# Six key-difference tasks 36 slots apart instead of eight 24 slots apart, weight pieces 24 slots apart, and other scan spacings, in a gated mix of attention and Fourier mixing

## The chip, the cores and the metric

The kernel runs on one core of a Trainium2 chip. The time is that of one execution on the device in microseconds (us), as the median of several runs. The engines are named as in the profile: PE multiplies matrices (PEld is its loading of weights), DVE is the vector engine, ACT the scalar (activation) engine, POOL the general-purpose engine, and SP is an engine that here only issues DMA transfers. Each engine runs its own queue of instructions strictly in the order in which they were written, and waits at an instruction until what it needs is there. ACT and POOL have DMA queues of their own.

## The reference, cut to what matters

The input `x` has 2048 rows of 512 numbers. Everything is float32.

```python
g = sigmoid((x * gate_w).sum(-1))
qkv = x @ wqkv                               # 32 heads of 16
p = softmax(q @ k.T * 16**-0.5)              # 2048 x 2048 for each head
a = (p @ v) @ wo
b = Cr @ (x @ Wr.T) - Ci @ (x @ Wi.T)        # Cr, Ci: 2048 x 2048; Wr, Wi: 512 x 512
out = g * a + (1 - g) * b
```

The projection weights are 64 times larger than usual, so the softmax needs the maximum of each row of scores before it takes exponents. The kernel therefore computes every score twice: once in a *scan* that keeps only maxima, and once for use.

## The kernel before, in words

**Precision.** The matrix engine takes a rounded 32-bit format. To keep accuracy an operand is split into a rounded part `hi` (ACT copies and so rounds) and a rest `lo` (POOL or DVE subtracts `hi` from the number), and a product is three products: hi·hi, hi·lo and lo·hi.

**Slots.** The first part of the program, the front, is written out as *products*, each of which is a pair of 64-row matmuls that run side by side (`halves_of`, L176). After each pair `beside` (L225) is called: that is one *slot*. A block of output, 128 rows by 512, takes 12 slots (24 matmuls). `beside` does two more things. It runs what is due: `after(n, f, ...)` (L203) puts a piece of work on a list, and the work is written into its engine's queue n slots later, in the order of due slot. And it writes scans at a set rate: `scan_at(s)` sets the spacing in slots. A scan of 128 queries against 512 keys for two heads is a pair of matmuls with 48 rows. It costs the matrix engine as much as one slot.

**Stages of the front**, by slot count: q projections up to slot 240, k projections to 384 (`project_t`, L366), values to 576 (`wv`), the two hidden Fourier products to 768 (`wr`) and to 960 (`wi`) (`project_s`, L394), and then the sequence Fourier product in 96 units of 12 slots to 2112. After the front come the exponents and the product with the values for all heads, with the rest of the scans, which the change does not touch.

**A block's way out.** In `project_s` the matmuls of a block leave two halves in a pair of PSUM banks, `xy`, of which there are two. ACT copies the halves to `tx` (one buffer) and `ty` (two buffers), L401 and L402. Four slots later POOL adds them to `ab` (L498), and seven slots after that SP stores `ab` to memory. In `project_t` the sum `s` is made by POOL, ACT rounds it to `eh`, POOL subtracts to `el`, and SP stores both; for keys SP also stores the plain sum to `ks_d` (L388), and for odd blocks of 512 rows `kf_d` as well.

**Weights.** `load_w` (L338) loads one 512x512 weight matrix in a single transfer and splits it in four pieces, the first `wait` slots later and the others each 12 slots after the one before: ACT rounds (L281), POOL subtracts (L282). Pieces fall at multiples of 12 slots.

**Folded scans.** From scan 192 to 691 (`FOLDED`) keys come in pairs. Each scan multiplies the queries either with the difference of two key blocks or with the second block; then max(a, b) = max(a - b, 0) + b. ACT takes max(., 0) of the difference (L153), and DVE adds the other and keeps the maximum (L155). Their rate is PACE/FOLD_PACE over the spacing that `scan_at` set: with spacing PACE one folded scan falls each FOLD_PACE slots. With spacing NARROW it is slower, and this holds in the first 24 slots of the sequence product and around the *swap*, the 120 slots from 1656 to 1776, in which the operand of the real part is replaced by that of the imaginary part, one of 16 pieces after the other (`renew`, L575: ACT rounds, DVE or POOL subtracts).

**Key differences.** `fold_keys(f, g)` (L348) makes the differences for one quarter `f` of the heads and one pair of key blocks. SP loads the two sums from `ks_d` into `a` and `b` (two buffers in all, the tag `el`), POOL subtracts (after 12 slots), ACT rounds to `fh` (17), POOL subtracts the rest into the buffer of `b` (18), and SP stores both to `kf_d` (19 and 23). The next task's load of `b` has to wait until the last store has read that buffer. There are eight such tasks, 24 slots apart, all in the `wr` stage; the first is written at slot 594. `load_scan_beside` (L217) reads what was stored, for the first time at slot 835. Quarter 3 of the heads is never scanned in folded form: the last folded scan, 691, belongs to pair 10 of the 16, and a quarter has four pairs.

Of the kernel before, what the change touches and what calls it, by code (L numbers as in the profile page):

```python
# [10 lines left out]
F32 = mybir.dt.float32  # L11
# [13 lines left out]
NB = S // P  # L25
ND = D // P
# [9 lines left out]
FRONT = 564 + 16 * LATER  # L36
PACE = 3.9
FOLDED = range(3 * SCANS, FRONT)
FOLD_PACE = 2.23
NARROW = 4.5  # L40
NWARM = 20
MIX = TOTAL - FRONT + 1
OUT = MIX + NB * LATER
# [3 lines left out]
def build(tc, x, xT, wqkv, wo, wrT, wiT, cr, ci, gate, out):  # L47
    nc = tc.nc
    with ExitStack() as ctx:
# [140 lines left out]
        with ExitStack() as pf:  # L190
# [8 lines left out]
            def xy():  # L199
                ps = psf.tile([P, 2, 512], F32, tag="xy", name="xy")  # L200
                return ps[:, 0, :], ps[:, 1, :]

            def after(n, f, *args):  # L203

                count[0] += 1
                due.append((slots[0] + n, count[0], f, args))
# [15 lines left out]
            def scan_at(spacing):  # L222
                pace[0] = spacing

            def beside():  # L225
# [3 lines left out]
                if pace[0] is None:  # L229
                    return  # L230
                pace[1] += (PACE / FOLD_PACE if seen[0] in FOLDED else 1.0) / pace[0]
                if seen[0] == FOLDED[0] and not beds:
# [39 lines left out]
            def products(ps, parts):  # L272
                n = 0
                for lhs, rhs in parts:
                    for a, b in ((0, 0), (0, 1), (1, 0)):
                        halves_of(ps, lhs[a], rhs[b], n == 0, n == 3 * len(parts) - 1)
                        n += 1
                        beside()
# [5 lines left out]
            def load_operand(ph, s, pool):  # L284
                raw = pool.tile([P, D], F32, tag="raw", name="abr", bufs=3)
                nc.sync.dma_start(raw, ab_d[ph][s])
                return raw
# [14 lines left out]
            def load_coef(n, raw):  # L302
                ph, t, u = coef[n]
                craw[n] = raw
                nc.sync.dma_start(raw, (cr, ci)[ph][t, :, u * CS:(u + 1) * CS, :])
# [11 lines left out]
            with ExitStack() as px:  # L317
# [20 lines left out]
                def load_w(w, src, wait, engine):  # L338

                    raw = stk.tile([P, ND, 512], F32, tag="stk", name="wraw")  # L340
                    nc.sync.dma_start(raw, src.rearrange("(d p) m -> p d m", p=P))
                    for d in range(ND):
                        after(wait + 12 * d, split_w, w, d, raw[:, d, :], engine)

                def split_x(d, c):
                    split(*xs[d, c], raws[d][:, c * 512:(c + 1) * 512], nc.vector)
# [1 line left out]
                def fold_keys(f, g):  # L348

                    a, b = (ep.tile([P, 512], F32, tag="el", name="fa") for _ in range(2))  # L350
                    c = 2 * g
                    for i, v in enumerate((a, b)):
                        nc.sync.dma_start(v, ks_d[f][:, (c + i) * 512:(c + i + 1) * 512])
                    hi = ep.tile([P, 512], F32R, tag="gb", name="fh", bufs=1)
                    lo = b.bitcast(F32R)

                    def store(i, v):
                        nc.sync.dma_start(kf_d[f][:, i, c * 512:(c + 1) * 512], v.bitcast(F32))

                    after(12, nc.gpsimd.tensor_sub, a, a, b)  # L360
                    after(17, nc.scalar.copy, hi, a)
                    after(18, nc.gpsimd.tensor_sub, lo, a, hi.bitcast(F32))
                    after(19, store, 0, hi)
                    after(23, store, 1, lo)

                def project_t(w, dst, f, c, ps=None):  # L366
                    ps = ps or xy()
                    products(ps, [([w[i][d][:, f * P:(f + 1) * P] for i in range(2)], xs[d, c])
                                  for d in range(ND)])
                    tx = ep.tile([P, 512], F32, tag="tx", name="tx", bufs=1)  # L370
                    folded = dst is k_d
                    s = ep.tile([P, 512], F32, tag="ty", name="s")
                    hi = ep.tile([P, 512], F32R, tag="eh", name="eh", bufs=3)
                    lo = ep.tile([P, 512], F32R, tag="el", name="el")
                    nc.scalar.copy(tx, ps[0])
                    if pace[0] is None:
                        after(5, nc.vector.tensor_add, s, ps[1], tx)
                    else:
                        nc.scalar.copy(s, ps[1])
                        after(5, nc.gpsimd.tensor_add, s, s, tx)  # L380

                    def store(i, v):
                        nc.sync.dma_start(dst[f][:, i, c * 512:(c + 1) * 512], v.bitcast(F32))
                        if folded and c % 2:
                            nc.sync.dma_start(kf_d[f][:, i, c * 512:(c + 1) * 512], v.bitcast(F32))

                    if folded:
                        after(10, nc.sync.dma_start, ks_d[f][:, c * 512:(c + 1) * 512], s)  # L388
                    after(9, nc.scalar.copy, hi, s)
                    after(10, nc.gpsimd.tensor_sub, lo, s, hi.bitcast(F32))  # L390
                    after(14, store, 0, hi)
                    after(20, store, 1, lo)

                def project_s(w, t, sign, use):  # L394
                    ps = xy()
                    q = slice((t % 4) * P, (t % 4 + 1) * P)
                    products(ps, [([v[:, q] for v in xs[d, t // 4]], [w[i][d] for i in range(2)])
                                  for d in range(ND)])
                    tx = ep.tile([P, 512], F32, tag="tx", name="tx", bufs=1)
                    ty = ep.tile([P, 512], F32, tag="ty", name="ty")  # L400
                    nc.scalar.mul(tx, ps[0], sign)  # L401
                    nc.scalar.mul(ty, ps[1], sign)  # L402
                    after(4, use, t, tx, ty)
# [43 lines left out]
                for n, (w, dst, f, c) in enumerate(order):  # L447
                    lead = s1() if n in (0, 2, 4, 6) else None
                    project_t(w, dst, f, c, lead and (lead[:, 0, :], lead[:, 1, :]))
# [3 lines left out]
                    project_t(wq, q_d, f, c)  # L453
                wv = new_w()
                for n, (f, c) in enumerate([(f, c) for f in range(1, ND) for c in range(NC)]):
                    if n == 3:
                        load_w(wv, wqkv[:, 1024:1536], 48, nc.gpsimd)
                    project_t(wk, k_d, f, c)

# [35 lines left out]
                def to_rhs(i):  # L495
                    def use(t, tx, ty):
                        ab = ep.tile([P, 512], F32, tag="eh", name="ab", bufs=3)
                        nc.gpsimd.tensor_add(ab, tx, ty)  # L498
                        after(7, nc.sync.dma_start, ab_d[i][t], ab)
                    return use  # L500

                for t in range(NB):
                    if t == 3:
                        load_w(wi, wiT, 48, nc.gpsimd)
                    if t % 2:
                        after(6, fold_keys, *divmod(t // 2, 2))
                    project_s(wr, t, 1.0, to_rhs(0))
                use = to_rhs(1)
                for t in range(NB):
                    if t > 3:  # L510
                        after(24, split_operand, t - 4, load_operand(0, t - 4, rp), nc.gpsimd)
                    if t == 8:
                        first = stk.tile([P, 4, CS, P], F32, tag="stk", name="first")
                        tail = stk.tile([P, 4, D], F32, tag="stk", name="tail")
                    if 8 <= t < 12:
                        load_coef(t - 8, first[:, t - 8])
                    if t >= 12:
                        nc.sync.dma_start(tail[:, t - 12, :], ab_d[0][t])
                    if t == 12:
                        scan_at(5.0)  # L520
                    if 12 <= t < 15:
                        after(4, prepare, t - 12, nc.scalar.copy, nc.vector.tensor_sub)
                    project_s(wi, t, -1.0, use)
                run_due(True)

            with ExitStack() as py:
# [9 lines left out]
                for d in range(4):  # L536
                    after(4 + 6 * d, split_operand, NB - 4 + d, tail[:, d, :], nc.vector if d < 2 else nc.gpsimd)
                scan_at(NARROW)
                after(24, scan_at, PACE)
# [9 lines left out]
                for n, (ph, t, u) in enumerate(coef):  # L549
                    prepare(n + 3)  # L550
                    fetch(n + 8)
                    if u == 0 and (ph, t) == (0, NB - 1):
                        scan_at(NARROW)
                    if u == 2 and (ph, t) == (1, 0):
# [6 lines left out]
                    hi, lo = ready.pop(n)  # L561
# [5 lines left out]
                    if (ph, t, u) == (0, NB - 3, 0):  # L567
                        for i in range(2):
                            raw = stk.tile([P, 4, D], F32, tag="stk", name="early")
# [437 lines left out]
```

## Time and profile before

| | |
|---|---|
| runs shown | median 1776.61 us (1775.0 to 1776.8) |
| profiled execution | 1772.7 us, of it 1770.9 us from the first to the last instruction |
| PE busy | 97% of the span |
| ACT, DVE, POOL busy | 82%, 65%, 40% |
| front: slots 0 to 2112 | about 5.8 to 717 us |
| values to the wr stage | slot 384 at 118.3 us, slot 576 at 175.7 us |
| wr stage, wi stage | slots 576 to 768 at 175.7 to 253.6 us, to 960 at 313.7 us |
| swap | slots 1656 to 1776 at 554.2 to 599.2 us |

The times of slots are read by counting the matmuls of L180 in the trace, two to a slot. In the profile, a share of PE busy near 100% says little by itself, as matmuls overlap; the number of matmuls or weight loads in a stretch says more. In the view by windows each engine has its busy time and, in brackets, the number of its instructions. In the chain of work that ended last, each line is a start, a length and what it was: an engine with the tile that it wrote and its line, or a DMA with what it moved. In the lists of waits, a line names who waited for whom, the sum in us, how often, and the longest one.

### The profile page before, as it was taken

How to read it: one execution, taken by the hardware profiler on the slowest of the kernel's cores; microseconds unless marked ns; L12 is line 12 of the kernel's file. 1: busy time of each engine (PE TensorE's matmuls, PEld its weight loads, DVE VectorE, ACT ScalarE, POOL GpSimd, SP SyncE). 2: the span in 40 equal slices, each digit the busy share in tenths (PEclk: the TensorE clock that was granted, in tenths of full speed). 3: DMA queues.
4: the chain of work that ended last, by engine and by line, in shares of the span. 5: the costliest groups of instructions: out<-in, count | busy, mean ns of one | idle time of the engine just before them, and what ended most of it. 6: DMA issues, size and time to landing. Idle time of an engine off the chain costs nothing.

```text
span 1770.9 us, 35629 instructions
## 1 busy us (share of the span) xinstructions
PE 1724.9 (97%) x13640; PEld 1032.9 (58%) x13640; DVE 1151.2 (65%) x1876; ACT 1451.5 (82%) x2386; POOL 716.4 (40%) x818
## 2 busy tenths in 40 slices
PE   8999879999999999999999999999999999999998
PEld 6877658898898788434333333333334555555554
DVE  6799869889989898666666666666664221122333
ACT  5445234788888788899999999999999888888885
POOL 3678556655555665123232323323232322222212
PEclk9999999999999999999999999999999999999999
DMA  8693657433335546341433332414413253254712
GB/s 296 216 335 89 190 156 220 132 113 107 114 121 180 155 129 136 69 74 29 93 59 61 58 66 55 88 35 78 90 31 71 69 118 91 70 137 123 183 42 98
DMA packets 128538, 202.69 MB, mean 114 GB/s; under 512 B 54208, under 2 KB 56752, under 8 KB 121456
## 3 DMA queue, kind: packets, MB, share of 16 engines
q1 hardware_dynamic: 86096, 164.17, 34.3%
q0 software_dynamic: 38496, 19.47, 5.2%
q10 hardware_dynamic: 3776, 16.78, 3.5%
q8 instruction: 107, 1.75, 0.4%
q14 instruction: 63, 0.52, 0.1%
HBM read 134.09 MB, written 65.81 MB: 113 GB/s over the span
## 4 chain that ended last, share of the span: by engine, by line
PE 86%; DMA 6%; DVE 2%; POOL 2%; issue 2%; ACT 1%; SPq 0%; DVEq 0%; POOLq 0%; ACTq 0%
PE pvb L658 28%; PE xy L180 20%; PE s L643 18%; PE s L180 8%; PE s L149 7%; PE s L130 6%; DMA fa<-ks_d 2%; DMA kf_d<-fa 1%; POOL fa L215 1%; DVE mx L132 1%; DMA raws<-xT 1%; DMA ks_d<-s 1%; DMA raws<-wqkv 0%; DMA q_d<-el 0%; POOL s L215 0%
## 5 line engine op out<-in xcount | busy, mean ns | idle before, releaser
L132 DVE TENSOR_REDUCE mx<-s 128x2 f32<-128x1024 f32 x524 | 628.8, 1223 | 228.9 <-PE s L130 227.7
L647 ACT ACTIVATE eb<-s 128x1024 f32<-128x1024 f32 x512 | 581.7, 1136 | 54.4 <-PE s L643 54.4
L651 ACT ACTIVATE e<-s 128x512 f32<-128x512 f32 x1024 | 612.7, 713 | 0.4 <-PE s L643 0.4
L658 PE MATMUL pvb<-e,va 128*17 128x512 f32 x2048 | 516.9, 598 | 0.0
L658 PE MATMUL pvb<-eb,va 128*17 128x512 f32 x2048 | 516.7, 598 | 0.0
L643 PEld LDWEIGHTS s<-qs,ks 50*128 50x128 f32 x2048 | 213.8, 185 | 372.3 <-ACT eb L647 282.6
L643 PE MATMUL s<-qs,ks 50*128 50x512 f32 x2048 | 427.8, 437 | 2.3 <-DVE ty L598 1.6
L155 DVE CUSTOM_DVE_ANT_0 fold<-s,fold 128x512 f32<-128x512 f32 x500 | 336.9, 690 | 42.2 <-PE s L149 20.0
L153 ACT ACTIVATE fold<-s 128x512 f32<-128x512 f32 x500 | 294.3, 602 | 70.0 <-PE s L149 51.4
L149 PE MATMUL s<-ks,qs 48*128 48x512 f32 x1000 | 236.0, 403 | 7.2 <-DVE mx L155 5.7
L130 PE MATMUL s<-ks,qs 48*128 48x512 f32 x1048 | 221.8, 398 | 4.4 <-DVE mx L132 2.9
L666 POOL DMA_DIRECT2D lc<-ob x124 | 62.9, 514 | 303.3 <-DVE ob L663 303.3
L658 PEld LDWEIGHTS pvb<-eb,va 128*17 128x17 f32 x2048 | 69.1, 95 | 188.3 <-issue 180.3
L149 PEld LDWEIGHTS s<-ks,qs 48*128 48x128 f32 x1000 | 129.0, 184 | 40.9 <-DVE mx L155 16.2
L673 POOL DMA_DIRECT2D r_d<-lc x31 | 18.1, 583 | 292.5 <-DVE lc L672 282.5
L130 PEld LDWEIGHTS s<-ks,qs 48*128 48x128 f32 x1048 | 107.8, 185 | 15.2 <-DVE mx L132 5.7
L180 PE MATMUL xy<-w,b 64*128 64x512 f32 x768 | 107.1, 396 | 2.7 <-ACT ty L402 2.4
L675 POOL DMA_DIRECT2D rb<-r_d x124 | 60.3, 494 | 68.7 <-DMA r_d<-lc 68.5
L180 PEld LDWEIGHTS xy<-w,b 64*128 64x128 f32 x768 | 74.9, 188 | 19.6 <-ACT ty L402 4.0
L752 DVE SCALAR_TENSOR_TENSOR y<-s,g,y 128x512 f32<-128x512 f32 x50 | 36.6, 748 | 76.4 <-PE s L180 75.8
L180 PE MATMUL s<-b,chi 64*128 64x512 f32 x542 | 85.2, 390 | 0.3 <-ACT chi L961 0.3
L401 ACT ACTIVATE tx<-xy 128x512 f32<-128x512 f32 x48 | 28.7, 597 | 65.9 <-PE xy L180 48.1
(750 smaller groups left out, 2365.8 us busy)
## 6 DMA issues: line engine op xcount, KB each, us to landing
craw<-ci SPq DMA_DIRECT2D x64, 256.0 KB
craw<-cr SPq DMA_DIRECT2D x60, 256.0 KB
ks<-k_d SPq DMA_DIRECT2D x46, 256.0 KB
qs<-q_d SPq DMA_DIRECT2D x46, 256.0 KB
ab_d<-ab SPq DMA_DIRECT2D x32, 256.0 KB
y_d<-y SPq DMA_DIRECT2D x32, 256.0 KB
o_d<-oh POOLq DMA_DIRECT2D x28, 256.0 KB, 9.4
o_d<-ol POOLq DMA_DIRECT2D x28, 256.0 KB, 12.7
```

What stands on the lines that cost most here:

```text
L130: nc.tensor.matmul(ps[:, j, :], qs[b:b + 48, qb * P:(qb + 1) * P], ks[b:b + 48, c * 512:(c + 1) * 512], start=True, stop=True)
L132: nc.vector.tensor_reduce(mx[p][:, :, qb, c], ps, axis=AX.X, op=ALU.max)
L149: nc.tensor.matmul(ps, qs[b:b + 48, qb * P:(qb + 1) * P], ks[b:b + 48, c * 512:(c + 1) * 512], start=True, stop=True)
L153: nc.scalar.activation(fold[j], ps, AF.Relu)
L155: nc.vector.tensor_tensor_reduce(out=fold[j], in0=ps, in1=fold[j], scale=1.0, scalar=-3.0e38, op0=ALU.add, op1=ALU.max, accum_out=mx[p][:, ...
L180: nc.tensor.matmul(ps[j], lhs[r], rhs[r], start=first, stop=last)
L643: nc.tensor.matmul(pss[j], ks[b:b + 50, kb * P:(kb + 1) * P], qs[b:b + 50, q0:q0 + 512], start=True, stop=True)
L647: nc.scalar.activation(e, ps, AF.Exp, scale=SCALE)
L651: nc.scalar.activation(e[j], pss[j], AF.Exp, scale=SCALE)
L658: nc.tensor.matmul(pvb[r:r + VC, :], va[:, kb, 2 * p + j, :], es[c][j], start=kb == 0, stop=kb == NB - 1, tile_position=(0, r))
L666: nc.gpsimd.dma_start(lc[32 * n:32 * n + 32, :], ob[r + DH:r + VC, :].rearrange("p (s e) -> p s e", e=16))
L675: nc.gpsimd.dma_start(rb[r:r + DH, :], r_d[p][h][n:n + 1, :].to_broadcast([DH, 512]))
```

## The change

Six things are edited.

- `fold_keys` is called six times, not eight: quarter 3 is left out, and five tasks are written in the `wr` stage at every third block, the sixth at the first block of the `wi` stage. They are 36 slots apart; the first stays at slot 594.
- In a task the subtraction is queued 14 slots after the load (12 before), the rounding 22 (17), the second subtraction 24 (18), the stores 28 and 31 (19 and 23).
- The plain sums of the keys of quarter 3 are no longer stored to `ks_d`: four transfers of 256 KB less in the k stage.
- Pieces of the weights of the `wv`, `wr` and `wi` products are split 24 slots apart (12). The load of the value weights is written two blocks earlier, at slot 252 instead of 276, so its pieces fall at slots 300, 324, 348 and 372 instead of 324, 336, 348 and 360.
- FOLD_PACE is 2.19 (2.23): one folded scan each 2.19 slots.
- NARROW is 5.3 (4.5): at the swap one folded scan each 2.98 slots instead of 2.57.

```diff
-FOLD_PACE = 2.23
-NARROW = 4.5
+FOLD_PACE = 2.19
+NARROW = 5.3
...
                     for d in range(ND):
-                        after(wait + 12 * d, split_w, w, d, raw[:, d, :], engine)
+                        after(wait + 24 * d, split_w, w, d, raw[:, d, :], engine)
...
-                    after(12, nc.gpsimd.tensor_sub, a, a, b)
-                    after(17, nc.scalar.copy, hi, a)
-                    after(18, nc.gpsimd.tensor_sub, lo, a, hi.bitcast(F32))
-                    after(19, store, 0, hi)
-                    after(23, store, 1, lo)
+                    after(14, nc.gpsimd.tensor_sub, a, a, b)
+                    after(22, nc.scalar.copy, hi, a)
+                    after(24, nc.gpsimd.tensor_sub, lo, a, hi.bitcast(F32))
+                    after(28, store, 0, hi)
+                    after(31, store, 1, lo)
...
-                    if folded:
+                    if folded and f < ND - 1:
                         after(10, nc.sync.dma_start, ks_d[f][:, c * 512:(c + 1) * 512], s)
...
-                    if n == 3:
+                    if n == 1:
                         load_w(wv, wqkv[:, 1024:1536], 48, nc.gpsimd)
...
-                    if t % 2:
-                        after(6, fold_keys, *divmod(t // 2, 2))
+                    if t % 3 == 1 and t < NB - 1:
+                        after(6, fold_keys, *divmod(t // 3, 2))
                     project_s(wr, t, 1.0, to_rhs(0))
...
+                    if t == 0:
+                        after(6, fold_keys, 2, 1)
                     project_s(wi, t, -1.0, use)
```

## The prediction

> **What bounds the kernel now.** I read the page first, then the windows cut at the stages that the change touches, then the chain and the waits inside the worst of them.
>
> ```profile
> PE 1724.9 (97%) x13640; PEld 1032.9 (58%) x13640; DVE 1151.2 (65%) x1876; ACT 1451.5 (82%) x2386; POOL 716.4 (40%) x818
> ```
>
> By the page PE is the bound, 97% busy. The change takes no matmul away, so it can win only where PE stands still. How much that is, the number of weight loads (the x behind PEld) tells, better than busy time:
>
> ```profile
> core 0: us, PE busy (x) PEld busy (x) DVE busy (x) ACT busy (x) POOL busy (x), PEclk, DMA share, GB/s
> 271.89:299.87 27.98, 27.98 (x243) 24.27 (x240) 27.98 (x26) 12.49 (x23) 18.57 (x15) 1.00 0.86 243
> 182.67:271.89 89.22, 71.53 (x546) 54.73 (x544) 67.25 (x63) 25.84 (x49) 48.10 (x38) 0.92 0.57 173
> 101.22:118.30 17.08, 15.17 (x124) 11.38 (x120) 14.94 (x14) 7.93 (x15) 14.15 (x12) 1.00 0.92 285
> 139.73:147.69 7.96, 7.75 (x65) 5.64 (x62) 7.96 (x9) 4.41 (x10) 7.77 (x7) 1.00 0.28 72
> 357.00:546.00 189.00, 188.83 (x1603) 170.78 (x1601) 170.28 (x513) 156.17 (x270) 101.63 (x104) 1.00 0.41 126
> 554.15:599.20 45.05, 42.01 (x337) 32.74 (x335) 40.53 (x112) 36.57 (x67) 28.20 (x27) 1.00 0.49 149
> ```
>
> The first stretch (slots 816 to 912) runs without a hole: 240 loads in 27.98 us, 0.1166 us each, 0.233 us a pair. At that price the others should take:
> - slots 600 to 816, with the eight key-difference tasks: 544 x 0.1166 = 63.4; they take 89.2. **25.8 us lost.**
> - slots 336 to 384, the end of the k stage: 14.0 of 17.1, 3.1 lost.
> - slots 456 to 480 (values): 7.2 of 8.0, 0.7 lost.
> - the swap, slots 1656 to 1776: 39.1 of 45.05, 6.0 lost.
> - the steady folded stretch: 186.7 of 189.0, 1% lost; there is nothing to win there.
>
> What holds PE in the first of these, the chain shows:
>
> ```profile
> 181.77 5.70 DMA fa<-ks_d
> ...
> 190.91 6.14 DMA kf_d<-fa
> 197.12 3.15 DMA fa<-ks_d
> ...
> 203.71 2.19 DMA kf_d<-fa
> 205.92 3.25 DMA fa<-ks_d
> ...
> 214.43 2.00 DMA kf_d<-fa
> 216.45 3.44 DMA fa<-ks_d
> ```
>
> PE isn't on it at all. A task's load, two subtractions and store run one after the other, and the next load waits for the store, as both use one buffer. The loop from load to load is 10.5 us (205.92 to 216.45), while 24 slots with their scans need 24 x 4.9/3.9 x 0.233 = 7.0 us of PE. The waits show how that reaches PE:
>
> ```profile
> ACT fh L215 <- POOL fa L215: 43.8, 8, 8.5
> POOL fa L215 <- DMA fa<-ks_d: 20.5, 7, 5.8
> PEld xy L180 <- ACT ty L402: 20.3, 10, 4.1
> ```
>
> POOL stands at the first subtraction until the load is there, 20.5 us in all. ACT stands at the rounding until POOL is done (43.8), and the rounding, 17 slots after a task that starts 6 slots into a block, is queued in slot 11 of a block, just ahead of the block's own copies out of PSUM. Those come late, and PE finds no free bank (20.3).
>
> **The change, part by part.**
>
> *Key-difference tasks: -23.8 us.* The period becomes 36 slots: 36 x 0.293 = 10.5 us of PE. What the loop needs comes from the rows above and these:
>
> ```profile
> L498 POOL TENSOR_TENSOR ab<-tx,ty 128x512 f32<-128x512 f32 x18 | 23.2, 1287 | 11.3 <-ACT ty L402 11.3
> L215 POOL TENSOR_TENSOR fa<-fa,fh 128x512 fp32r<-128x512 f32 x8 | 10.2, 1273 | 4.4 <-ACT fh L215 4.4
> L282 POOL TENSOR_TENSOR w<-wraw,w 128x512 fp32r<-128x512 f32 x4 | 5.1, 1284 | 2.5 <-ACT w L281 2.5
> ```
>
> Load 3.25, subtraction 1.27, one block's add that now falls between the subtractions 1.29 (the rounding runs beside it), second subtraction 1.27, store 2.2: 9.3 us, 10.6 where a weight piece comes between as well. So the loop fits into 10.5. POOL's own load fits too: in 36 slots three adds, two subtractions and at most two pieces, 7 x 1.28 = 9.0 (it was two adds, two subtractions and two pieces in 7.0: 7.7). The rounding moves to slot 4 of a block, behind the block's copies, so a late load no longer holds those.
>
> The first task stays bad: by the slots, the loads for a scan (from 586 on) and the 1 MB of the next weights (612) are issued around it as before, and its load took 5.70 and its store 6.14. With these its loop is 5.70 + 1.27 + 1.29 + 1.27 + 6.14 = 15.7, so the second load is 5.2 us late. SP stands at it; behind it is a block's store, which can wait, since `ab` has three buffers. POOL's subtraction is queued 14 slots (4.1 us) after the load, so POOL stands 5.2 + 3.2 - 4.1 = 4.3 us. Before PE feels that, the add may be 1.0 us late (due 4 slots into a block of 3.5 us, 1.29 long, wanted by the next block's copy) and the copies 2.4 (1.1 long, wanted a block later): 3.4. That leaves 0.9 us. The lateness then shrinks by up to 1.2 us a task, and where a weight piece is queued too, a few tenths more slip through: I take 2.0 us lost in place of 25.8. The bounds: 0 (everything hidden) and, if each task had the first one's transfers, nothing gained (the second rival). The two tasks left out take 4 loads, 4 stores, 4 subtractions and 2 roundings away; they are in the count. The sixth task, at slot 774, stands near where the eighth stood (762), ahead of the `split_operand` work; `kf_d` is first read at slot 835, and then of quarter 0.
>
> *Weight pieces, k stage: -0.8 us (0 to -2).*
>
> ```profile
> 106.32 1.29 POOL L215 TENSOR_TENSOR s<-s,tx 128x512 f32<-128x512 f32 x1
> 109.58 1.29 POOL L282 TENSOR_TENSOR w<-wraw,w 128x512 fp32r<-128x512 f32 x1
> 110.82 1.29 POOL L215 TENSOR_TENSOR s<-s,tx 128x512 f32<-128x512 f32 x1
> ...
> 115.32 1.30 POOL L215 TENSOR_TENSOR s<-s,tx 128x512 f32<-128x512 f32 x1
> ...
> 118.58 1.29 POOL L215 TENSOR_TENSOR s<-s,tx 128x512 f32<-128x512 f32 x1
> ```
>
> A block with a piece takes POOL 4.50 us (106.32 to 110.82), one without 3.26 (115.32 to 118.58); PE needs 3.5. Four pieces in a row put POOL 4.0 behind, of which 3.1 reached PE, so 0.9 is hidden. With a piece in every second block POOL falls 1.0 behind and wins 0.24 back: from the second piece on some 0.75 each reaches PE, 2.3 in all. Two blocks with one piece still need 7.76 of 7.0, so half a cure. The four `ks_d` stores and the earlier weight load relieve a stretch at 285 GB/s; I count nothing for it, since the waits there end with POOL. The last piece, at slot 372, has 21 slots before its first matmul.
>
> *Weight pieces, values: -0.7 us (0 to -0.7).*
>
> ```profile
> L474 POOL TENSOR_TENSOR va<-tx,ty 128x512 f32<-128x512 f32 x15 | 19.4, 1294 | 9.2 <-ACT ty L402 9.1
> L470 POOL TENSOR_TENSOR xg<-xn,gb 128x512 f32<-128x512 f32 x14 | 18.1, 1292 | 0.0
> ```
>
> Add 1.29, gate product 1.29 and a piece 1.28 are 3.9 for a block of 3.5; with a piece in every second block it is 6.4 for 7.0, and POOL keeps up.
>
> *Swap: -3.0 us (0 to -5).* Counting the slots, 40 scans fall into it instead of 47.
>
> ```profile
> L155 DVE CUSTOM_DVE_ANT_0 fold<-s,fold 128x512 f32<-128x512 f32 x48 | 32.2, 686 | 4.8 <-ACT fold L153 2.6 <-PE s L149 1.4
> L215 DVE TENSOR_TENSOR b<-early,b x6: 684/688/1415, 557.3 to 570.7; 128x512 fp32r<-128x512 f32 x6
> L153 ACT ACTIVATE fold<-s 128x512 f32<-128x512 f32 x47 | 27.6, 605 | 6.6 <-PE s L149 6.1
> L578 ACT CAST b<-abr 128x512 fp32r<-128x512 f32 x8 | 5.1, 633 | 1.9 <-DMA abr<-ab_d 1.9
> ```
>
> DVE has 40.5 us of work there against PE's 39.1, so it sets the pace. Seven scans fewer take 7 x 0.67 (32.2/48) = 4.7 off DVE (35.8), 7 x 0.59 = 4.1 off ACT's 36.6 (32.5) and 7 x 0.233 = 1.6 off PE (37.4): PE leads again. What stays is ACT's wait for a reloaded operand, 1.9, and about 1 of order: 3.0 of 6.0. The seven scans cost PE the same elsewhere.
>
> The twelve operand subtractions on DVE (six of them in the row above: shortest 0.68 us, median 0.69, longest 1.42) could also come to lie beside POOL's more often than now. If each took a POOL subtraction's 1.28 us more, DVE's work would be 35.8 + 15.4 = 51 us, 12 over the 39.1 of PE now, and this part would lose 6 instead of winning 3. The Trainium skill, SBUF — State Buffer, section "SBUF: two separate sides", has a rule that speaks for this: a DVE instruction with two SBUF inputs and a POOL instruction that reads SBUF exclude each other, and the second to start waits until the first has ended. The trace agrees with it in the longest, 1.42, but the median of 0.69 says that it seldom strikes here; the sum would be 1748.6 by the row and 1757.6 by the rule in full.
>
> *FOLD_PACE 2.19: +0.3 us (0 to +1).* PE's period of a scan falls from 3.23 to 3.19 pairs, 0.753 to 0.744 us; DVE's work for one in the steady stretch is 170.3/248 = 0.687 (1601 loads make 248 scans). It stays below; the 2.3 us lost there grow a little. The start of the sequence product, with 8 scans instead of 9 in 24 slots, I leave at nothing.
>
> **Sum.** -23.8 - 0.8 - 0.7 - 3.0 + 0.3 = -28.0. The profiled execution took 1772.7 (span 1770.9), which would be 1744.7; the median shown stands 3.9 above it, so on its scale 1776.6 - 28.0 = 1748.6. The stages after the front start earlier and are otherwise as they were.
>
> **The rivals.**
>
> *The loop still holds PE now and then* (1753 to 1763). For it: two later rounds have a load of 4.27 and a store of 3.98 (below). With both the loop is 4.27 + 3 x 1.28 + 3.98 = 12.1, 1.6 over the period; six tasks lose 9.6 beside the first one's 0.9, not 2.0 in all: 1757. Against it: the stores shown above after the first took 2.19 and 2.00.
>
> ```profile
> 234.27 3.98 DMA kf_d<-fa
> ...
> 255.95 4.27 DMA fa<-ks_d
> ```
>
> *Slower: transfers stretch as PE's pace packs them closer.* The place is SP's queue at the load of `b`. If each task had the first one's 5.70 and 6.14, and the weight pieces between, the loop would be 17.0 and six tasks 102 us, against 89.2 now: +12.8, less the 4.2 of the other parts, 1785. It decides from a loop of 16.2 us on (6 x 16.2 = 97.2, 3.5 us or 0.2% above today after the other gains). Against it: in 36 slots a task's four transfers and three blocks' stores, 7 x 256 KB, make 1.8 MB in 10.5 us, 171 GB/s, and the stretch moves 173 today.
>
> *The swap doesn't gain*, since ACT's wait for a reloaded operand, not the scans, sets it: 1751.6. Every subtraction there held up by POOL: 1757.6; against it, the median of the six above lies at their shortest.
>
> *Better than forecast:* the loop hidden fully, k stage and swap at their bounds, -33.2: 1743.4.
>
> **How the numbers follow.** About 0.2%, 3.5 us, is what a measurement tells from no change. Forecast, with or without a gain at the swap, 1743 to 1753: 70%. Loop still felt, 1753 to 1763: 15%. DVE's subtractions all held up: 4%. Below 1743: 4%. Gains smaller yet, 1763 to 1773: 3%. Same 1%, slower 3%. Range 1743 to 1761, which holds about eight in ten; faster 0.96, same 0.01, slower 0.03.
>
> **What would show it.** Right: 182 to 272 us of before shrinks to about 65; ACT's wait for POOL `fa` falls from 43.8 to under 15; the chain there is PE; in the swap DVE has about 36 us of work, and PE loses 3. Wrong: loads of `fa` waiting on `kf_d` stores in every task, PE waiting on ACT `ty` for over 8 us, or DVE holding PE between 320 and 550 us.

## The result and the profile after

The changed kernel takes 1751.4 us (median; 1750.5 to 1756.7) against 1775.8 us before: a ratio of 0.987, 95% interval 0.985 to 0.989. That is 24.4 us faster by the medians, 1 to 1.5%; 28.0 us were forecast, at 1748.6, in a range of 1743 to 1761. The profiled execution took 1751.4 us, its span 1749.6 instead of 1770.9. All stages are read as in the prediction: the time of a stretch, less 0.1166 us for each weight load that starts in it, is what PE lost (the view counts one or two more, at the edges).

The page's line of PE, and the windows of the same slots as before:

```profile
PE 1719.9 (98%) x13640; PEld 1021.8 (58%) x13640; DVE 1155.1 (66%) x1876; ACT 1451.9 (83%) x2384; POOL 712.7 (41%) x814
```

```profile
core 0: us, PE busy (x) PEld busy (x) DVE busy (x) ACT busy (x) POOL busy (x), PEclk, DMA share, GB/s
533.02:577.17 44.15, 40.84 (x323) 33.93 (x321) 38.12 (x98) 32.79 (x62) 28.39 (x27) 0.96 0.45 142
246.91:274.88 27.97, 27.97 (x242) 22.67 (x240) 27.97 (x26) 12.27 (x23) 18.73 (x16) 1.00 0.86 252
179.62:246.91 67.29, 64.52 (x547) 50.79 (x544) 65.95 (x63) 25.46 (x47) 42.71 (x34) 1.00 0.65 195
100.82:115.07 14.25, 14.25 (x123) 12.60 (x120) 14.25 (x14) 7.41 (x14) 11.33 (x10) 1.00 0.96 303
136.68:144.64 7.96, 7.74 (x66) 5.64 (x63) 7.96 (x9) 3.90 (x9) 6.52 (x6) 1.00 0.26 72
298.55:533.02 234.47, 233.24 (x1961) 202.20 (x1958) 213.35 (x631) 194.71 (x336) 127.36 (x129) 1.00 0.42 122
```

In order: the swap, the clean stretch (27.97 for 240 loads, as before), the key-difference tasks (67.3 us for 544 loads instead of 89.2), the end of the k stage (14.25 instead of 17.08), the values at slots 456 to 480 (7.96, as before), and slots 984 to 1656 (234.5 for 1958 loads, which should take 228.3).

In the stage of the tasks, the chain and the waits are:

```profile
178.72 5.28 DMA fa<-ks_d
187.97 7.39 DMA kf_d<-fa
195.42 3.25 DMA fa<-ks_d
202.61 4.17 DMA kf_d<-fa
206.84 3.14 DMA fa<-ks_d
```

```profile
POOL fa L215 <- DMA fa<-ks_d: 13.9, 6, 3.2
ACT fh L215 <- POOL fa L215: 13.0, 6, 3.2
PEld xy L180 <- ACT ty L402: 2.8, 3, 1.9
```

The first task's transfers are as slow as they were (5.28 and 7.39), the next store is slow too (4.17), and after the third load the chain is PE. ACT's wait for POOL fell from 43.8 to 13.0, and PE's wait for the copies from 20.3 to 2.8. PE's granted clock in the stretch rose from 0.92 to 1.00: before, it stood at half for 13.65 us behind the holes, in which PE was busy for 11.75 us with 60 loads that take 7.0 at the full clock. So some 4.8 of the 25.8 us were lost clock, and the rest was standing still.

What PE lost, stage by stage, in us. The experiments' rows are explained below. Where nothing that bears on a stage was edited, 456 to 480 and 1776 to 2088 repeat within 0.1 from kernel to kernel, 984 to 1656 within 0.4, 336 to 408 within 0.5, and the swap with the old spacings lies between 5.7 and 6.4. Slots 600 to 816 scatter most (2.2 to 4.4 with the new tasks, 25.8 to 28.5 with the old ones).

| kernel | 336-408 | 456-480 | 600-816 | 984-1656 | swap | 1776-2088 |
|---|---|---|---|---|---|---|
| before | 3.2 | 0.7 | 25.8 | 3.0 | 6.1 | 4.2 |
| changed | 0.9 | 0.7 | 3.9 | 6.2 | 6.8 | 3.2 |
| tasks alone | 3.4 | 0.7 | 2.3 | 3.0 | 5.7 | 4.2 |
| pieces alone | 0.9 | 0.7 | 28.5 | 3.0 | 6.4 | 4.2 |
| spacings alone | 3.4 | 0.7 | 26.7 | 6.1 | 6.9 | 3.3 |
| changed, old spacings | 0.9 | 0.7 | 3.7 | 2.9 | 5.7 | 4.2 |
| early load alone | 1.5 | 0.7 | 27.1 | 2.9 | 6.1 | 4.2 |
| maxima apart | 0.9 | 0.7 | 2.2 | 5.6 | 8.2 | 4.4 |
| maxima beside | 0.9 | 0.7 | 2.2 | 8.3 | 6.0 | 5.3 |
| apart, NARROW 4.5 | 1.3 | 0.7 | 4.3 | 4.8 | 5.9 | 2.4 |
| apart, four buffers | 0.9 | 0.7 | 2.8 | 5.6 | 2.0 | 4.3 |
| the same, NARROW 4.5 | 0.8 | 0.7 | 3.1 | 5.1 | 4.8 | 2.4 |
| all together | 0.8 | 0.7 | 4.4 | 4.3 | 2.1 | 3.0 |

Two things stand out in the second row: the tasks and the k stage gained, and the scan spacings lost. At the swap, where 3 us were to be won, 0.7 was lost (0.4 to 1.1 against the five kernels with the old spacings), and slots 984 to 1656 lose 3.2 more.

### The profile page after: what moved, and what is told of

Read it like the earlier page. It is cut to its first block, busy times and chain, and to the rows that moved or that the text cites. A ratio compares the mean times of both kernels' runs of the same rounds, so it can differ in the third digit from the quotient of the medians.

```text
span 1749.6 us, 35589 instructions
## 1 busy us (share of the span) xinstructions
PE 1719.9 (98%) x13640; PEld 1021.8 (58%) x13640; DVE 1155.1 (66%) x1876; ACT 1451.9 (83%) x2384; POOL 712.7 (41%) x814
## 4 chain that ended last, share of the span: by engine, by line
PE 89%; DMA 3%; DVE 3%; POOL 2%; issue 2%; ACT 1%; SPq 0%; DVEq 0%; ACTq 0%; POOLq 0%
PE pvb L660 28%; PE xy L180 21%; PE s L645 19%; PE s L180 8%; PE s L149 7%; PE s L130 6%; DVE mx L132 1%; DMA fa<-ks_d 1%; DMA kf_d<-fa 1%; POOL s L215 1%; DMA raws<-wqkv 0%; DMA raws<-xT 0%; POOL el L215 0%; POOL fa L215 0%; DMA abr<-ab_d 0%
## 5 line engine op out<-in xcount | busy, mean ns | idle before, releaser
L149 PE MATMUL s<-ks,qs 48*128 48x512 f32 x1000 | 223.3, 404 | 7.6 <-DVE mx L155 6.1
L130 PE MATMUL s<-ks,qs 48*128 48x512 f32 x1048 | 221.6, 396 | 3.7 <-DVE mx L132 2.5
L149 PEld LDWEIGHTS s<-ks,qs 48*128 48x128 f32 x1000 | 120.9, 184 | 47.6 <-DVE mx L155 18.2
L130 PEld LDWEIGHTS s<-ks,qs 48*128 48x128 f32 x1048 | 108.3, 184 | 14.9 <-DVE mx L132 6.0
```

The lines of the kernel that those rows point to most:

```text
L130: nc.tensor.matmul(ps[:, j, :], qs[b:b + 48, qb * P:(qb + 1) * P], ks[b:b + 48, c * 512:(c + 1) * 512], start=True, stop=True)
L149: nc.tensor.matmul(ps, qs[b:b + 48, qb * P:(qb + 1) * P], ks[b:b + 48, c * 512:(c + 1) * 512], start=True, stop=True)
```

## The experiments

### Which part does what

Four kernels: the tasks alone, the weight pieces with the earlier load alone, the two spacings alone, and the changed kernel with the old spacings.

```diff
# spacings alone, in the kernel before
-FOLD_PACE = 2.23
-NARROW = 4.5
+FOLD_PACE = 2.19
+NARROW = 5.3
```

**Tasks alone** (in the changed kernel, the 12 slots between pieces, the load at n == 3 and the old spacings put back):

> The kernel before with the six key-difference tasks, their new delays and the four ks_d stores left out; weight pieces and scan spacings as before. Theory A (the stages add up as the two traces have them): the tasks are nearly the whole gain, -22 us against before; slots 600 to 816 take 67 to 69 us instead of 89.2, the k stage (slots 336 to 384) stays at about 17 us. Rival B (the tasks' gain needs the pieces 24 slots apart, since POOL would otherwise be too full): -15 us or less, slots 600 to 816 take 74 us or more.

Measured: 1752.1 us, ratio to before 0.988 (0.986 to 0.989), and the tasks' slots lose 2.3 instead of 25.8. The tasks are nearly the whole gain. They don't need the pieces 24 slots apart: rival B is out. The k stage loses 3.4, as without the edit, so the four stores to `ks_d` that this kernel leaves out bring nothing that shows there.

**Pieces alone:**

> The kernel before with the weight pieces 24 slots apart and the value weights loaded two blocks earlier, nothing else. Theory A: slots 336 to 408 lose 0.9 us instead of 3.2, -2.5 us against before in all; the 0.7 us lost at slots 456 to 480 stay, as DVE and not POOL loses them. Rival C (the step of the prediction: POOL's budget alone decides): -0.8 us in the k stage and -0.7 us at slots 456 to 480.

Measured: 1772.7 us, ratio 0.9995 (0.9986 to 1.0004). The k stage gains as theory A had it, 3.2 to 0.9, and the values nothing. But the whole is not 2.5 us faster, since slots 600 to 816 lose 28.5 instead of 25.8. How much of that comes from the pieces is open: two other runs with the old tasks have 26.7 and 27.1 there.

**Spacings alone:**

> The kernel before with FOLD_PACE 2.19 and NARROW 5.3, nothing else. Theory A (the row maxima's small DVE instructions now fall beside POOL's subtractions and wait for them): +2 us against before (0 to +4); slots 1680 to 1704 take 11 us instead of 8.2, and two blocks at slots 1392 and 1536 lose 1 us or more. Rival D (the prediction: the swap gains as DVE has fewer scans): -2.7 us, the swap takes 41 us instead of 45.

Measured: 1777.3 us, ratio 1.0021 (1.0009 to 1.0033). They make the kernel slower, in the places that theory A named: slots 1680 to 1704 lost 3.8 us, the 24 slots from 1392 and from 1536 1.5 and 1.1. The swap takes 44.2 us, not 41.

**The changed kernel with the old spacings:**

> The changed kernel with FOLD_PACE 2.23 and NARROW 4.5 put back. Theory A: 1 to 3 us faster than the changed kernel, -24 us against before (1751 to 1749). Rival D: 3 us slower than the changed kernel, -21 us or less against before.

Measured: 1749.0 us, ratio to before 0.986 (0.984 to 0.988), 2.4 us under the changed kernel by the medians, though the two intervals overlap. The stages are clearer, and they are as theory A had them: 2.9 and 5.7 where the changed kernel loses 6.2 and 6.8.

### Why the spacings lose: small instructions beside POOL's

When a pair's scans are done, four DVE instructions work on its maxima (`shift`, L158): a maximum, a transpose, a rounding (L172) and a rest (L173), each on 32 numbers a partition. The spacing decides in which slot they fall. The pair that ends at the swap ended at slot 1680 before and at 1671 after. DVE there, and POOL at the same time, in the changed kernel (start, length, instruction):

```profile
543.02 1.27 DVE L172 CAST chi<-mt 128x32 fp32r<-128x32 f32 x1
...
544.82 1.09 DVE L215 TENSOR_TENSOR b<-early,b 128x512 fp32r<-128x512 f32 x1
545.84 1.25 DVE L173 TENSOR_TENSOR clo<-mt,chi 128x32 fp32r<-128x32 f32 x1
```

```profile
542.96 1.30 POOL L215 TENSOR_TENSOR b<-early,b 128x512 fp32r<-128x512 f32 x1
544.76 0.61 POOL L313 CAST chi__8571<-craw 128x512 fp32r<-128x512 f32 x1 [0.50 <-PE xy L180]
545.45 1.59 POOL L314 TENSOR_TENSOR clo__8572<-craw,chi__8571 128x512 fp32r<-128x512 f32 x1
```

The rounding of 32 numbers starts 0.06 us after a POOL subtraction and ends 0.03 after it: 1.27 us. Each of the two small ones costs DVE over a microsecond, the scans behind them wait, and PE stands. Slots 1680 to 1704 in the changed kernel:

```profile
541.08:552.25 11.17, 9.57 (x68) 8.07 (x66) 10.36 (x25) 6.97 (x14) 5.85 (x6) 0.86 0.36 120
```

They lose 3.7 us, where the kernel before loses 0.5. PE stood still for 1.6 us in its longest hole there, and behind it ran at half its clock for 3.41 us (the mean is 0.86), with 17 loads in the time of 29; that is some 1.4 of the 3.7.

To test this, the same four instructions were moved, once to where POOL has nothing to do, once to where it has.

```diff
-                        for d, part in enumerate(shift(done // SCANS)):
-                            after(3 + 4 * d, part)
+                        parts, k = shift(done // SCANS), 3
+                        while done >= FOLDED[0] and ((slots[0] + k - 960) % 48 != 28 or
+                                                     55 <= (slots[0] + k - 960) // 12 < 72):
+                            k += 1
+                        if done == 511:
+                            k = 1776 + 4 - slots[0]
+                        at = (0, 1, 2, 3, 7) if done >= FOLDED[0] else (0, 4, 8, 12, 16)
+                        for d, part in zip(at, parts):
+                            after(k + d, part)
```

For *beside*, 28 is 2, the first of `at` is (0, 2, 6, 11, 15), and the pair of the swap goes to slot 1778.

> The changed kernel with one edit: the four small DVE instructions that end a pair's folded scans (maximum, transpose, rounding, rest) are put into slots 4 to 7 of a unit in which POOL has nothing but the coefficients' split, which is over by then; for the pair that ends at the swap, after the swap. Theory A (these instructions wait beside POOL's subtractions, and the change moved them there): slots 984 to 1656 lose 3.5 us instead of 6.2 and the swap 3.0 to 3.5 instead of 6.8, about 6 us faster than the changed kernel (1745); the rounding and the rest take 0.2 us each everywhere. Rival E (the denser scans themselves, with less left of DVE's time, lose it): slots 984 to 1656 lose 5.5 us or more, under 1.5 us faster.

> The changed kernel with the same four instructions put so that the rounding and the rest fall beside POOL's add of a block and its split, for six of seven pairs (after the swap for the other). Theory A: each of the six pairs costs 1 to 1.5 us; slots 984 to 1656 lose 7 to 9 us (five of the pairs end there), the swap 3.0 to 3.5, and rounding and rest take about 1.1 us each. Rival E: as with these instructions apart, within 1 us.

The rounding and the rest of the seven pairs (shortest, median and longest in ns), in the changed kernel, apart, and beside:

```profile
L173 DVE TENSOR_TENSOR clo<-mt,chi x8: 182/190/1249, 289.9 to 655.3; 128x32 fp32r<-128x32 f32 x8
...
L172 DVE CAST chi<-mt x7: 175/185/1275, 345.9 to 653.6; 128x32 fp32r<-128x32 f32 x7
```

```profile
L172 DVE CAST chi<-mt x7: 175/181/183, 349.9 to 656.3; 128x32 fp32r<-128x32 f32 x7
L173 DVE TENSOR_TENSOR clo<-mt,chi x7: 186/192/194, 350.1 to 656.5; 128x32 fp32r<-128x32 f32 x7
```

```profile
L172 DVE CAST chi<-mt x7: 177/1077/1154, 359.2 to 667.0; 128x32 fp32r<-128x32 f32 x7
L173 DVE TENSOR_TENSOR clo<-mt,chi x7: 189/787/1292, 360.8 to 668.6; 128x32 fp32r<-128x32 f32 x7
```

The mechanism is shown: apart, none takes over 0.2 us, and the three bad stretches of 24 slots in the changed kernel (from 1392, 1536 and 1680) fall from 1.5, 1.0 and 3.7 us to 0.3, 0.3 and 0.7. Beside, the median rounding takes 1.08 us, and slots 984 to 1656 lose 8.3 instead of 5.6.

But the time did not follow. Apart: 1750.6 us, ratio 0.986 (0.984 to 0.988), 0.9 under the changed kernel instead of 6, and not to be told from it. Beside: 1753.7, ratio 0.988 (0.986 to 0.989); its swap loses 6.0, not 3.0 to 3.5. Two things took the gain.

First, slots 984 to 1656 still lose 5.6 us, which is rival E's number. PE's waits there, before and with the instructions apart (sum in us, times, longest):

```profile
PEld s L149 <- DVE mx L155: 2.8, 13, 0.6
PEld s L149 <- ACT fold L153: 1.7, 6, 0.4
```

```profile
PEld s L149 <- DVE mx L155: 6.3, 27, 0.5
PEld s L149 <- ACT fold L153: 3.9, 13, 0.4
```

At 2.19 slots a scan there are twice as many short waits for DVE and ACT as at 2.23, none over 0.5 us. Of the 3.2 us lost more in the changed kernel, 2.1 stood in the two stretches beside POOL and came back when these were cleared. But the moved instructions cost something at their new places: the units from slots 1128, 1272, 1416 and 1560, into which four pairs' instructions now fall, lose 0.3 us each, 1.3 in all, and nothing before or in the changed kernel. They are written there in four successive slots instead of four slots apart; no run tells whether that is why. So only about 1.1 to 1.3 us of the loss are left for the denser scans, and rival E is right for that much.

Second, the swap: it loses 8.2 us now, 6.3 of them in its last 24 slots.

### What was late next at the swap

With the small instructions apart, the last 24 slots of the swap (windows, waits, and the chain):

```profile
562.85:576.57 13.72, 10.48 (x66) 8.00 (x64) 6.01 (x18) 5.23 (x10) 5.07 (x6) 0.75 0.40 129
```

```profile
ACT b L587 <- DMA abr<-ab_d: 4.0, 1, 4.0
```

```profile
560.17 6.52 DMA abr<-ab_d
```

The same load in the chain of the kernel before and of the changed one:

```profile
586.20 4.71 DMA abr<-ab_d
```

```profile
565.26 4.75 DMA abr<-ab_d
```

The last of the sixteen operands is reloaded through three buffers. Its load is issued when a buffer is free, behind a store of results, a load of coefficients and the next block's load, and takes 6.5 us. ACT waits for it 1.9 us before, 2.2 in the changed kernel and 4.0 here. From 2.2 to 4.0 it is the transfer itself that grew, by 1.8 us; what made it longer is open, since the DMA share while it ran was no higher than in the other two (0.83 against 0.87). The hole costs PE's clock too: 0.75 on the mean in these 13.7 us, as PE stood for 3.24 us and then ran at half its clock for 6.83. The Trainium skill, TensorE: Matmul & The Clock Gate, section "Part 1: The HAM clock gate (the "warmup" mystery)", says that the array falls to half its clock after some 3.4 us of idleness and regains it after as long a busy stretch. The trace agrees in kind, but less was enough here: in the changed kernel the 3.41 us at half clock came behind a stretch whose longest hole was 1.59 us.

Three more kernels, all with the small instructions apart: two with four such buffers (`AHEAD` is 4, `bufs` a new argument of `load_operand`), so that the last load is issued one piece earlier, with NARROW at 5.3 and 4.5; and, with three buffers, one with NARROW at 4.5:

```diff
-                raw = pool.tile([P, D], F32, tag="raw", name="abr", bufs=3)
+                raw = pool.tile([P, D], F32, tag="raw", name="abr", bufs=bufs)
...
-                        if s >= 8 and s + 3 < NB:
-                            early[s + 3] = load_operand(1, s + 3, cp)
+                        if s >= 8 and s + AHEAD < NB:
+                            early[s + AHEAD] = load_operand(1, s + AHEAD, cp, AHEAD)
...
-                                for i in range(8, 11):
-                                    early[i] = load_operand(1, i, cp)
+                                for i in range(8, 8 + AHEAD):
+                                    early[i] = load_operand(1, i, cp, AHEAD)
```

> The changed kernel with the four instructions apart from POOL's, and NARROW back at 4.5, FOLD_PACE 2.19. Theory A with the prediction's reading of the swap (DVE has more work than PE there at the denser spacing): the swap loses 5.0 to 6.0 us, 2 to 3 more than with NARROW 5.3 and the same four apart. Rival F (the swap's loss is ACT's wait for a reloaded operand and order, not the number of scans): it loses 3 to 3.7, the same within 0.5.

> The kernel with the four small instructions apart (NARROW 5.3, FOLD_PACE 2.19), and the swap's reloaded operands with four buffers in place of three, so that the last one is issued one piece earlier, ahead of the next block's load. Theory H (with the small instructions out of the way the last reload is what the swap waits for): ACT's wait for it falls from 4.0 to under 1 us, the swap loses 2 to 3 us instead of 8.2, about 5.5 us faster than with the instructions apart alone (1745). Rival I (the reload is slow wherever it is issued, as the transfers jam there): ACT still waits 3 us or more, the swap loses 7 or more.

> The same with NARROW 4.5. Theory J (the prediction's reading of the swap, right once nothing else holds it: at the denser spacing DVE has more work than PE): the swap loses 4.5 to 6 us, 2 to 3.5 more than with NARROW 5.3. Rival F (not the number of scans): the same within 0.7.

With three buffers and NARROW 4.5 (1748.6 us, ratio 0.985, 0.984 to 0.987), the swap loses 5.9, less than the 8.2 at 5.3, so as a whole it is neither F nor A. But only 1.2 of the 5.9 stand in the last 24 slots, against 6.3 of the 8.2; ahead of them the sparser scans lose 1.9 and the denser 4.7, which is A's difference. With four buffers, the whole swap at 5.3 and at 4.5:

```profile
532.94:572.21 39.27, 38.83 (x324) 32.55 (x322) 35.90 (x94) 32.59 (x62) 27.89 (x27) 1.00 0.49 158
```

```profile
532.06:575.77 43.71, 42.23 (x337) 33.35 (x334) 40.30 (x108) 36.54 (x68) 27.43 (x26) 1.00 0.49 150
```

At 5.3 ACT has no wait for the reload any more, DVE has 35.9 us of work beside PE's 37.3 (320 loads start in the stretch), and the swap loses 2.0, as theory H had it. At 4.5 DVE has 40.3 beside 38.9 (334 loads), and it loses 4.8. So the sparser scans are worth 2.8 us at the swap, once nothing else holds it. The times: 1748.3 us, ratio 0.985 (0.984 to 0.987), where 1745 was expected, and 1746.4, ratio 0.984 (0.983 to 0.985); the second is no slower, since with NARROW 4.5 the scans end earlier and the stretch after the swap loses 2.4 instead of 4.3.

### The k stage

In the kernel before, the transfer of the value weights alone is issued 24 slots earlier; the pieces stay in their slots.

```diff
-                    if n == 3:
-                        load_w(wv, wqkv[:, 1024:1536], 48, nc.gpsimd)
+                    if n == 1:
+                        load_w(wv, wqkv[:, 1024:1536], 72, nc.gpsimd)
```

> The kernel before with one edit: the transfer of the value weights is issued at slot 252 instead of 276; its four pieces stay at slots 324, 336, 348 and 360. Theory G (the transfer jams the key stores, POOL waits for one of them, and enters the pieces 2 us late): slots 336 to 408 lose 1.0 to 1.8 us instead of 3.2. Rival C (only POOL's budget counts): 3.0 to 3.3 as before.

Measured (a single run, 1774.0 us): slots 336 to 408 lose 1.5 us instead of 3.2. Up to slot 456 it is 2.4 instead of 3.5, against 0.9 with the pieces spread as well, so the load brings 1.1 of the 2.6, and the spread pieces 1.5. POOL before, and with the early load:

```profile
92.77 1.29 POOL L215 TENSOR_TENSOR el<-s,eh 128x512 fp32r<-128x512 f32 x1 [2.88 <-DMA kf_d<-el]
```

```profile
93.54 1.29 POOL L215 TENSOR_TENSOR el<-s,eh 128x512 fp32r<-128x512 f32 x1 [0.73 <-ACT eh L215]
```

Before, POOL stood 2.88 us for a key store that was late beside the 1 MB transfer, ahead of the first piece. With the early load it waits only for the rounding, 0.73, as in any block. The same wait is 5.07 us in the kernel with the tasks alone and 3.91 in that with the spacings alone, which have the late load, and it is missing in the changed kernel and in the one with the pieces alone, which have the early one.

### All together

Maxima apart, four buffers, the gate's small DVE instructions moved to the start of the sequence product, FOLD_PACE 2.22 and NARROW 5.2:

> The instructions apart, four reload buffers, the gate's small DVE instructions moved from the wr stage to the start of the sequence product, FOLD_PACE 2.22 and NARROW 5.2. Theory A with H: slots 984 to 1656 lose 3 to 4 us, the swap 2 to 3, slots 600 to 816 a little less than 2.2; 1743, some 8 us faster than the changed kernel. Rival: 1747 to 1750, as the start's scatter and new collisions take it back.

Measured: 1745.8 us, ratio to before 0.984 (0.983 to 0.985), 5.7 us under the changed kernel by the medians, though the two intervals still touch. That lies between the 1743 of the theory and the 1747 to 1750 of its rival. The swap (2.1) is as expected, slots 984 to 1656 (4.3) lose a little more. The tasks' slots lose 4.4 instead of a little under 2.2, so moving the gate brought nothing that could be told from their scatter.

## Why the prediction was right, and where it was wrong

- **The tasks, -23.8: right, -21.9 in the changed kernel and -23.5 alone.** The loop of load, two subtractions and store held PE, and 36 slots let it run beside PE. 2.0 us were to remain; 2.2 to 4.4 do. The first task's slow transfers stay, as said, and from the third load on the loop fits; the second store, put at 2.2 us, took 4.17. What the prediction left out is the clock: some 4.8 of the 25.8 us were not waiting but work at half clock behind the holes, and they went with the holes.
- **The k stage, -0.8: right in kind, mis-sized.** Slots 336 to 408 won 2.3, and 2.6 up to slot 456. The step that failed is "I count nothing for it", of the earlier weight load: it kept a key store from being late and POOL from entering the pieces some 2 us behind, and brought 1.1. The prediction read POOL from 101 us on, and POOL's wait for the late store ends at 92.8. The pieces themselves brought 1.5 instead of 0.8.
- **The values, -0.7: wrong.** POOL's work in the stretch fell from 7.77 to 6.52 us and the 0.7 stayed to the hundredth. The waits there say who holds PE, the same in both kernels:

```profile
PEld s L130 <- DVE mx L132: 1.1, 2, 0.6
```

  DVE is busy all 7.96 us, before and after. POOL being over its budget was true, but not what PE waited for.
- **The swap, -3.0: wrong in the changed kernel (+0.7), right once two things were cleared (-2.8).** The step that DVE has more work than PE there and sets the pace held: outside slots 1680 to 1704 and the last 24, the changed kernel loses 1.3 us instead of 3.9. The step "What stays is ACT's wait for a reloaded operand, 1.9, and about 1 of order" failed: the maxima's instructions came to lie beside POOL's subtractions, and slots 1680 to 1704 lost 3.2 more, clock included. So DVE had 38.1 us of work and not 35.8; the two slow instructions make 2.2 of the difference. ACT's wait hardly changed (2.2), but with the instructions apart the reload took longer and cost 6.3.
- **POOL's lock on DVE.** The prediction put it as a rival at the operand subtractions. It struck there too (1.09 above, beside a rounding of POOL's) but mostly at the maxima's two instructions, which it did not name. The Trainium skill, SBUF — State Buffer, section "SBUF: two separate sides", has the rule that the later of the two waits until the first has ended; the trace agrees, at 1.27 us for an instruction that takes 0.18 alone.
- **FOLD_PACE, +0.3: mis-sized.** Slots 984 to 1656 lost 3.2 more, the stretch after the swap 1.0 less, the first 24 slots 0.5 less: +1.7. The term that was missing is again the maxima's instructions beside POOL, 2.1 of the 3.2. The denser scans themselves are left with about 1.1 in that stretch: the comparison of sums, 0.687 us of DVE against 0.744, had no place for the short waits, which were there before and doubled.
- **The sum.** The tasks -21.9, the k stage up to slot 456 -2.6, the swap +0.7 and the pace +1.7 make -22.1; the start gains 0.4 and what lies after slot 2088 loses 1.3 more, and the spans differ by 21.3. No edit touches what comes after the front; from slot 2088 to the end the thirteen profiles take 1062.0 to 1064.6 us. The medians differ by 24.4, as the profiled execution of before lay below its median and that of the changed kernel at it. By the spans the forecast of 28.0 was 6.7 too good: it promised 3.7 too much at the swap, 1.9 at the tasks, 1.4 at the pace, 0.7 at the values and 0.8 in the start and the rest, and 1.8 too little at the k stage. That the median came within 3 us of the forecast is luck in part: the k stage won what was not counted, and the medians differ by 3 us more than the spans. The measured 1751.4 also lies on the 1751.6 of the rival "the swap doesn't gain", but not for that rival's reason, as ACT's wait for the operand was not what took the gain there. One sum of another rival is slightly off: a loop of 16.2 us would put the time 3.8, not 3.5, above the kernel before.

## What to carry to other kernels

When a task off the critical path is a serial loop through DMAs, compare its length with PE's time for the same stretch, and count the slots behind it: a period just longer than the loop took away nearly all of its stall. When slots are shifted, look at which small instructions of one engine come to lie beside long ones of another; the sum of work doesn't show it. And after a stall is removed, look at the slack of the next transfer in line: here a reload that had cost under 2 us cost 6 when it came 1.8 us later. A hole costs more than its length when PE's clock falls behind it, so compare the granted clock as well as the waits.

## What the hardware showed that was not expected

- A DVE instruction on 32 numbers a partition takes 0.18 us alone and up to 1.29 beside a POOL instruction on 512, even the rounding, which has one input. The other way round a POOL subtraction that started while DVE's was running took 1.59 instead of 1.30.
- Of the transfers of 256 KB in the tasks' chain, those that ran at a DMA share of 0.50 to 0.80 took 2.0 to 4.3 us, and those at 0.93 to 0.99, around the loads of a scan's operands and of 1 MB of weights, 5.3 to 7.4 us.
- PE's clock fell to half for 3.41 us behind a stretch whose longest hole was 1.59 us, and for 6.83 us behind a hole of 3.24 us.
